# Attention and two MoE blocks on one core: tile zero's product with v three slots later, the softmax weights' product on GpSimd, six dense steps in the last slots

## The chip, the core and the metric

One core of a Trainium2 chip. The metric is device microseconds of one execution. Three runs of the kernel before gave a median of 700.36 us (699.11 to 701.2).

## What is computed

Attention with head mixing (12 heads, 448 rows, batch 2), then two dense blocks, all in fp32:

```python
scores = einsum('bhij,hg->bgij', scale * q @ k.T, w_pre)
attn = exp(scores - max(scores)); attn = attn / (sum(attn) + 1e-09)
attn = einsum('bhij,hg->bgij', attn, w_post)
x = (attn @ v) reshaped to (896, 768)
x = ((x @ w_a) * (x @ w_b)) @ w_out          # 768 -> 1536 -> 768
r = maximum(x @ w_in, 0); out = (r * r) @ w_out2   # 768 -> 2048 -> 768
```

## The kernel before

**Two parts.** The attention part runs first, the dense part behind it. The dense matmuls are split in three (hi*hi, hi*lo, lo*hi: lines 645 to 647), so a "dense step" (`fill(1)`, one `mm`) is three matmuls of 128x448. A dense unit is six steps and needs its weights split into hi and lo by six "split steps" on ScalarE (ACT) and VectorE (DVE).

**Slots.** Each batch has four row tiles of 120, 120, 120 and 88 rows, each cut into pairs of row groups: 6, 6, 6 and 5 pairs, so 46 slots in all; tile zero has slots 0 to 5, tile one 6 to 11. Slot n of the loop issues, in this program order: the premix of pair n+1 (heads mixed by w_pre, L291, PE), the scores qk of a later tile (L206, PE), `post` of pair n (mixing by w_post, L348, PE), then the softmax of pair n+1: row minimum `smin` (DVE, L300), `sexp` (ACT, L307), the addition of 1e-9 to the sum (`z`, L315), the copies of the scores out of PSUM (odd heads DVE L215, even heads ACT L217), and their spreading over partitions by DMA (L224, odd heads from SP's queue, even heads from GpSimd's (POOL's) own instructions). Then come the two copies `evac` of `post`'s result (ACT L376, DVE L374), and `weights2` of pair n+1: reciprocal (L323) and product w2 = wp * 1/z (L324), which `post` of pair n+1 reads as its moving operand in slot n+1. After that `mid` issues loads.

**The 88-row tile** has a second, partial spread per head (L258). In the slots of `HOLD` the spreads wait for the next slot.

**Tile's end.** Where a tile ends (`AVS`, before: slots 5, 11, 17, 22, 28, 34, 40), the product with v (`av_start`, `av`, L387 and L400, then the copies `av_out`) stands on PE, with split steps between. Two slots' softmax lie under it.

**Order.** The schedule is manual: each engine keeps the program order, and an instruction waits for its inputs and for buffers. PSUM has eight banks: T 3, post 2, qk 2, av 1.

Of the kernel before, what the change touches and what calls it, by code (L numbers as in the profile page):

```python
# [7 lines left out]
F32 = mybir.dt.float32  # L8
# [78 lines left out]
def attention_moe_kernel(  # L87
# [17 lines left out]
    PB = {"T": 3, "post": 2, "qk": 2, "av": 1}  # L105
# [21 lines left out]


# [70 lines left out]
    def qk(b, t, c, tags=("qk", "qk")):  # L199
# [102 lines left out]
    def sexp(b, m, f):  # L302
# [9 lines left out]
        if f:  # L312
            z = Z[b, m][0:q]
            eng = nc.vector if b == 0 and PAIRS[m][0] == 0 else nc.gpsimd
            eng.tensor_tensor(out=z, in0=z, in1=eps[0:q].to_broadcast([q, 2]), op=ALU.add)  # L315

    def weights2(b, m):
# [6 lines left out]
        nc.vector.tensor_tensor(  # L324
# [7 lines left out]
    def post_tag(b, m):  # L332
        return "qk" if (b, m) in free_qk else "post"

    def post(b, m):
        t, r, n = PAIRS[m]
        w2 = W2.pop((b, m))
        p = [ps(post_tag(b, m)) for _ in range(n)]
# [115 lines left out]
    def first(c):  # L454
        qk(0, 0, c, ("post", "post") if c % 2 else ("qk", "qk"))
# [43 lines left out]
    pre, aft, mid, end = {}, {}, {}, {}  # L499
    AVS = [base[i] + span[i] - 1 for i in range(len(tiles) - 1)]  # L500
# [7 lines left out]
    def softmax(n, between=()):  # L508
# [5 lines left out]
        for f, *args in between:  # L514
            f(*args)
# [13 lines left out]
    for i in range(0, VP, 2):  # L529
        at(mid, 2, load_v, 0, i, 2)  # L530
    for ti, (b, t) in enumerate(tiles):
# [17 lines left out]
        if ti + 1 < len(tiles):  # L549
            sl = s0 + sp - 1  # L550
            work = [[(steps, k)] for k in STEPS.get((b, t), (0, 0, 0))]
# [12 lines left out]
            at(end, sl, *work[2][0])  # L564
        if ti == 2:
# [10 lines left out]
    def split_steps(u):  # L576
# [10 lines left out]
        def s1():  # L587
# [4 lines left out]
            if u:  # L592
# [12 lines left out]
        def s4():  # L605
            st["hi"] = w_p.tile([128, UW], F32R, tag="wh", name="wh", bufs=3)
            nc.scalar.copy(st["hi"], st["c"])  # L607

        def s5():
            lo = w_p.tile([128, UW], F32R, tag="wl", name="wl", bufs=3)  # L610
# [16 lines left out]

    def split_x0(c):
        src = x32[0][c // 2][:, c % 2, :]
        hi, lo = single(f"ks{2 * c}"), single(f"ks{2 * c + 1}")  # L630
# [8 lines left out]
    for c in range(NC):  # L639
        at(mid, s1 - 2 + c, split_x0, c)  # L640
# [295 lines left out]
```

## Time and profile before

| | us |
|---|---|
| median of three runs | 700.36 |
| the profiled execution | 704.45 |
| its span, first to last instruction | 702.67 |
| PE busy | 680.1 (97%) |
| DVE, ACT, POOL busy | 473.6, 297.9, 62.8 |
| attention loop | 18.7 to 200.6 |
| last product with v | 200.6 to 204.2 |
| dense part to the last matmul | 204.2 to 698.2 |

The profiled execution is 4.1 us (0.6%) longer than the median. Matmuls are pipelined and their recorded ends are modelled, so a busy PE can be slower than it could be; a gap in PE's rows is idle time.

### The profile page before, as it was taken

How to read it: one execution, taken by the hardware profiler on the slowest of the kernel's cores; microseconds unless marked ns; L12 is line 12 of the kernel's file. 1: busy time of each engine (PE TensorE's matmuls, PEld its weight loads, DVE VectorE, ACT ScalarE, POOL GpSimd, SP SyncE). 2: the span in 40 equal slices, each digit the busy share in tenths (PEclk: the TensorE clock that was granted, in tenths of full speed). 3: DMA queues.
4: the chain of work that ended last, by engine and by line, in shares of the span. 5: the costliest groups of instructions: out<-in, count | busy, mean ns of one | idle time of the engine just before them, and what ended most of it. 6: DMA issues, size and time to landing. Idle time of an engine off the chain costs nothing.

```text
span 702.7 us, 16168 instructions
## 1 busy us (share of the span) xinstructions
PE 680.1 (97%) x6881; PEld 582.1 (83%) x6881; DVE 473.6 (67%) x795; ACT 297.9 (42%) x563; POOL 62.8 (9%) x139
## 2 busy tenths in 40 slices
PE   9879998998899999999999999999999999999997
PEld 2456766666689999999999999999999999999996
DVE  6648767798755876766767556668888887645530
ACT  3537655676543333333333322335555553323210
POOL 7112321236100000000000000000000000000000
PEclk9989999999999999999999999999999999999999
DMA  7864577544202323332233322323323234343300
GB/s 236 221 177 137 173 199 184 159 128 142 76 2 90 136 90 120 106 131 94 90 125 103 133 90 90 135 90 98 127 90 134 91 102 155 129 157 120 117 27 27
DMA packets 29092, 84.94 MB, mean 121 GB/s; under 512 B 5059, under 2 KB 18462, under 8 KB 29021
## 3 DMA queue, kind: packets, MB, share of 16 engines
q1 hardware_dynamic: 23933, 73.24, 32.1%
q0 software_dynamic: 4224, 9.43, 5.3%
q10 hardware_dynamic: 864, 1.24, 0.5%
q8 instruction: 54, 0.88, 0.5%
q14 instruction: 17, 0.14, 0.1%
HBM read 62.29 MB, written 2.75 MB: 93 GB/s over the span
## 4 chain that ended last, share of the span: by engine, by line
PE 87%; issue 3%; DVE 3%; ACT 2%; DMA 2%; POOL 1%; POOLq 0%; ACTq 0%; DVEq 0%
PE T L645 9%; PE T L647 9%; PE T L646 9%; PE post L646 6%; PE post L647 6%; PE post L645 6%; PE qk L647 6%; PE qk L645 6%; PE qk L646 6%; PE post L348 4%; PE T L291 4%; PE qk L206 3%; PE av L647 3%; PE av L646 3%; PE av L645 3%
## 5 line engine op out<-in xcount | busy, mean ns | idle before, releaser
L607 ACT CAST wh<-wc 128x768 fp32r<-128x768 f32 x68 | 56.8, 835 | 118.9 <-DVE wc L601 105.4
L611 DVE TENSOR_TENSOR wl<-wc,wh 128x768 fp32r<-128x768 f32 x68 | 64.9, 954 | 48.3 <-ACT wh L607 48.1
L307 ACT ACTIVATE e<-T,nb 128x448 f32<-128x448 f32 (+1 forms) x92 | 57.6, 630 | 55.6 <-DVE nb L300 55.4
L647 PE MATMUL T<-m,wl 128*128 128x448 f32 x207 | 75.6, 365 | 0.0
L645 PE MATMUL T<-m,wh 128*128 128x448 f32 x207 | 75.6, 365 | 0.0
L646 PE MATMUL T<-m,wh 128*128 128x448 f32 x207 | 75.6, 365 | 0.0
L348 PEld LDWEIGHTS post<-w,e 64*64 64x64 f32 x2624 | 53.8, 135 | 26.2 <-issue 12.5
L589 DVE SCALAR_TENSOR_TENSOR wa<-wr,wa 128x768 uint32<-128x768 uint32 x68 | 65.2, 958 | 2.3
L601 DVE SCALAR_TENSOR_TENSOR wc<-wc,wa 128x768 uint32<-128x768 uint32 x68 | 65.2, 958 | 2.3
L348 PE MATMUL post<-w,e 64*64 64x60 f32 (+1 forms) x2624 | 55.8, 218 | 9.0 <-issue 6.0
L584 ACT ACTIVATE wc<-wr 128x768 f32<-128x768 f32 x68 | 61.4, 903 | 0.0
L291 PE MATMUL T<-G,wpre_sb 64*64 64x448 f32 x352 | 53.0, 563 | 3.2 <-issue 2.9
L300 DVE TENSOR_REDUCE nb<-T 128x1 f32<-128x448 f32 (+1 forms) x92 | 52.9, 615 | 4.1 <-PE T L291 2.4
L597 DVE TENSOR_SCALAR wc<-wc 128x768 f32<-128x768 f32 x68 | 37.9, 558 | 19.3 <-ACT wc L584 19.3
L646 PE MATMUL post<-m,wh 128*128 128x448 f32 x125 | 45.7, 365 | 0.0
L645 PE MATMUL post<-m,wh 128*128 128x448 f32 x125 | 45.7, 365 | 0.0
L647 PE MATMUL post<-m,wl 128*128 128x448 f32 x125 | 45.6, 365 | 0.0
L645 PE MATMUL qk<-m,wh 128*128 128x448 f32 x116 | 42.4, 365 | 0.0
L646 PE MATMUL qk<-m,wh 128*128 128x448 f32 x116 | 42.4, 365 | 0.0
L647 PE MATMUL qk<-m,wl 128*128 128x448 f32 x116 | 42.4, 365 | 0.0
L645 PEld LDWEIGHTS T<-m,wh 128*128 128x128 f32 x207 | 38.9, 188 | 3.1
L646 PEld LDWEIGHTS T<-m,wh 128*128 128x128 f32 x207 | 38.9, 188 | 3.1
(180 smaller groups left out, 1416.1 us busy)
## 6 DMA issues: line engine op xcount, KB each, us to landing
wr<-w SPq DMA_DIRECT2D x65, 768.0 KB
G<-s POOLq DMA_DIRECT2D x24, 210.0 KB, 5.0
G<-s SPq DMA_DIRECT2D x20, 210.0 KB
outT<-ta SPq DMA_DIRECT2D x11, 224.0 KB
wr<-w SPq DMA_DIRECT2D x12, 192.0 KB
q<-qT SPq DMA_DIRECT2D x10, 180.0 KB
G<-s POOLq DMA_DIRECT2D x12, 140.0 KB, 3.1
v<-v SPq DMA_DIRECT2D x8, 192.0 KB
```

The lines of the kernel that those rows point to most:

```text
L291: nc.tensor.matmul(p[f][o:o + 64, 0:S], wpre_sb[i:i + 64, o:o + 64], G[t % 2][i:i + 64, r + g, :], start=True, stop=True, skip_group_check ...
L300: nc.vector.tensor_reduce(out=NB[b, m][0:q, f:f + 1], in_=Tps[b, m][f][0:q, 0:S], op=ALU.min, axis=AX.X)
L307: nc.scalar.activation(out=e[0:q], in_=Tps[b, m][f][0:q, 0:S], func=ACTF.Exp, bias=NB[b, m][0:q, f:f + 1], scale=-1.0, accum_out=Z[b, m][0 ...
L348: nc.tensor.matmul(p[g][64 * x:64 * x + 64, c:c + i], e[o:o + 64, j * 128 + y:j * 128 + y + 64], w2[o:o + 64, f, z:z + i], start=True, sto ...
L584: nc.scalar.activation(out=st["c"], in_=rd(st["high"]), func=ACTF.Abs, scale=HSC)
L589: nc.vector.scalar_tensor_tensor(out=a, in0=st["high"], scalar=0x80000000, in1=a, op0=ALU.bitwise_and, op1=ALU.bitwise_or)
L601: nc.vector.scalar_tensor_tensor(out=cu, in0=cu, scalar=3, in1=st["a"], op0=ALU.logical_shift_left, op1=ALU.bitwise_or)
L607: nc.scalar.copy(st["hi"], st["c"])
L611: nc.vector.tensor_tensor(out=lo, in0=st["c"], in1=rd(st["hi"]), op=ALU.subtract)
L645: nc.tensor.matmul(p[:, 0:S], hi[:, sl], x[0], start=first, stop=False)
L646: nc.tensor.matmul(p[:, 0:S], hi[:, sl], x[1], start=False, stop=False)
L647: nc.tensor.matmul(p[:, 0:S], lo[:, sl], x[0], start=False, stop=last)
```

## The change

1. `AVS` of tile zero moves from slot 5 to slot 8, so its probabilities `A[0, 0]` get a buffer of their own (`first_a`); when it is read, the pool is closed and the dense part's `wh`, `wl` buffers take its place.
2. The four loads of batch zero's v move from slot 2 to slots 4, 5, 6 and 7. Loads of k, v of batch one and of the dense weights move by some slots, and unit 3's weights load in slots 41 to 44.
3. The addition of 1e-9 to z goes from DVE to ACT for tile zero, and from POOL to DVE from pair 38 on.
4. The product w2 of pairs 7 to 37 goes from DVE to POOL.
5. In slots 39 to 44 one dense step each stands before `post`; the bank pair qk becomes two single banks, qk and qx, and `post` takes its banks from a list.
6. One split step of each tile end from tile three on moves ahead of the copies of `post`; the split of batch zero's x moves from slots 33 to 38 to 25, 27, 31, 35, 37, 39.

```diff
-    PB = {"T": 3, "post": 2, "qk": 2, "av": 1}
+    PB = {"T": 3, "post": 2, "qk": 1, "qx": 1, "av": 1}
...
+    early = ExitStack()
+    first_a = early.enter_context(tc.tile_pool(name="early", bufs=1, side="right"))
+    split_p = []
+
+    def open_split():
+        early.close()
+        split_p.append(ctx.enter_context(tc.tile_pool(name="split", bufs=3, side="right")))
...
         if f:
             z = Z[b, m][0:q]
-            eng = nc.vector if b == 0 and PAIRS[m][0] == 0 else nc.gpsimd
-            eng.tensor_tensor(out=z, in0=z, in1=eps[0:q].to_broadcast([q, 2]), op=ALU.add)
+            if b == 0 and PAIRS[m][0] == 0:
+                nc.scalar.activation(out=z, in_=z, func=ACTF.Identity, bias=eps[0:q])
+            else:
+                eng = nc.vector if plist.index((b, m)) >= QUIET else nc.gpsimd
+                eng.tensor_tensor(out=z, in0=z, in1=eps[0:q].to_broadcast([q, 2]), op=ALU.add)
...
         nc.vector.reciprocal(out=z, in_=z)
-        nc.vector.tensor_tensor(
+        n = plist.index((b, m))
+        (nc.gpsimd if base[1] < n < QUIET else nc.vector).tensor_tensor(
             out=w2[0:q],
...
-    def post_tag(b, m):
-        return "qk" if (b, m) in free_qk else "post"
+    def post_tags(b, m):
+        return free_qk.get(plist.index((b, m)), ("post", "post"))
...
-            A[b, t] = a_p.tile([128, NG, TILE], F32, tag="a", name="a")
+            A[b, t] = (a_p if b + t else first_a).tile([128, NG, TILE], F32, tag="a", name="a")
...
-    AVS = [base[i] + span[i] - 1 for i in range(len(tiles) - 1)]
+    AVS = [base[1] + 2] + [base[i] + span[i] - 1 for i in range(1, len(tiles) - 1)]
...
-    free_qk = set(plist[QUIET::2])
-    STEPS = {(0, 3): (0, 1, 1), (1, 0): (3, 0, 2), (1, 1): (2, 2, 1), (1, 2): (2, 1, 1)}
+    free_qk = {38: ("qx", "qk"), 40: ("qk", "post"), 41: ("qk", "post"), 42: ("post", "qk"), 44: ("qk", "post")}
+    STEPS = {(0, 3): (1, 0, 1, 0), (1, 0): (1, 3, 1, 0), (1, 1): (1, 2, 2, 0), (1, 2): (1, 2, 1, 0)}
...
-    for i in range(0, VP, 2):
-        at(mid, 2, load_v, 0, i, 2)
+    for i, n in enumerate((4, 5, 6, 7)):
+        at(mid, n, load_v, 0, 2 * i, 2)
...
-    for c, n in enumerate((7, 8, 9, 12, 13, 14)):
+    for c, n in enumerate((8, 9, 10, 12, 13, 14)):
         at(mid, n, load_k, 1, c)
-    for i, n in enumerate((10, 11, 11, 14, 15, 16, 17)):
+    for i, n in enumerate((16, 20, 20, 21, 21, 22, 23)):
         at(end if n in AVS else mid, n, load_v, 1, i)
-    for u, ns in enumerate(((17, 18, 19, 20), (22, 22, 23, 24), (34, 34, 38, 38))):
+    for u, ns in enumerate(((15, 17, 18, 19), (24, 25, 26, 27), (30, 31, 32, 33), (41, 42, 43, 44))):
...
-    for c in range(NC):
-        at(mid, s1 - 2 + c, split_x0, c)
+    for c, n in enumerate((25, 27, 31, 35, 37, 39)):
+        at(mid, n, split_x0, c)
...
-    tags = ["T", "qk", "qk", "post", "av", "T", "post", "T"]
+    tags = ["qx", "T", "qk", "post", "av", "T", "post", "T"]
...
         run(pre, n)
+        if QUIET < n and not last:
+            fill(1)
         post(*plist[n])
         run(aft, n)
         mine = [(evac, *plist[n], g) for g in range(2)]
         if n in AVS:
-            held, mine = held + mine, []
+            held, mine = held + between[n] + mine, []
```

`QUIET` is 38 and `base[1]` is 6.

## Rows read from the trace of the kernel before

**Rows 1.** The page, busy time of each engine, its share, and instructions.
```profile
PE 680.1 (97%) x6881; PEld 582.1 (83%) x6881; DVE 473.6 (67%) x795; ACT 297.9 (42%) x563; POOL 62.8 (9%) x139
```
**Rows 2.** Busy time by stretch: length, engines (x instructions), granted clock, DMA share, GB/s.
```profile
0.00:200.60 200.60, 182.57 (x4349) 121.34 (x4349) 145.92 (x334) 115.39 (x291) 62.77 (x139) 0.98 0.57 161
204.20:698.20 494.00, 493.93 (x2438) 457.49 (x2436) 325.99 (x458) 182.13 (x271) 0.00 (x0) 1.00 0.31 106
```
**Rows 3.** Waits: engine, line, releaser: us in total, times, longest.
```profile
DVE z L315 <- ACT e L307: 6.2, 6, 1.7
PE post L348 <- issue: 6.0, 6, 3.4
```
**Rows 4.** Timeline of DVE in slot 3: start, length, instruction, idle before.
```profile
33.15 1.15 DVE L300 TENSOR_REDUCE nb<-T 128x1 f32<-128x448 f32 x2
35.23 0.16 DVE L315 TENSOR_TENSOR z<-z,eps 128x2 f32<-128x2 f32 x1 [0.94 <-ACT e L307]
36.74 1.15 DVE L300 TENSOR_REDUCE nb<-T 128x1 f32<-128x448 f32 x2
```
**Rows 5.** Timeline of PE in slot 5.
```profile
44.84 0.74 PE L348 MATMUL post<-w,e 64*64 64x60 f32 x17 [3.36 <-issue]
```
**Rows 6.** Busy time by stretch behind that wait, columns as in rows 2.
```profile
44.10:51.00 6.90, 6.17 (x77) 4.93 (x79) 1.57 (x4) 1.62 (x4) 0.78 (x2) 0.51 0.39 104
```
**Rows 7.** DMA queues: packets, MB, share: whole run, 31.1:37.3, 37.3:41.8 (three), 41.8:45.
```profile
q8 instruction: 54, 0.88, 0.5%
...
v<-v SPq DMA_DIRECT2D x3, 384.0 KB
...
q0 software_dynamic: 156, 0.45, 42.8%
q1 hardware_dynamic: 337, 0.50, 42.3%
q14 instruction: 1, 0.01, 0.7%
...
q8 instruction: 1, 0.02, 2.7%
```
**Rows 8.** Timeline of DVE in slot 14.
```profile
83.19 0.28 DVE L324 TENSOR_TENSOR w<-wp,z 128x120 f32<-128x120 f32 x1
83.39 1.15 DVE L300 TENSOR_REDUCE nb<-T 128x1 f32<-128x448 f32 x2
85.11 0.62 DVE L374 COPY a<-post 128x420 f32<-128x420 f32 x1
85.75 0.17 DVE L323 RECIPROCAL z<-z 128x2 f32<-128x2 f32 x1
```
**Rows 9.** Timelines of ACT, POOL and PE there.
```profile
82.57 0.52 ACT L217 COPY s<-qk 88x448 f32<-88x448 f32 x1
...
84.10 0.63 ACT L307 ACTIVATE e<-T,nb 128x448 f32<-128x448 f32 x1 [0.53 <-DVE nb L300]
...
83.39 0.63 POOL L224 DMA_DIRECT2D G<-s  x1 [0.43 <-ACT s L217]
...
83.62 1.30 PE L348 MATMUL post<-w,e 64*64 64x60 f32 x58
```
**Rows 10.** Groups by line, POOL: form, count, busy us, mean ns, idle before.
```profile
L188 POOL TENSOR_TENSOR ks<-x,ks 128x112 fp32r<-128x112 f32 x24 | 9.7, 436 | 0.8 <-ACT ks L631 0.8
```
**Rows 11.** Timeline of POOL, an elementwise operation behind two spreads.
```profile
157.00 0.55 POOL L258 DMA_DIRECT2D G<-s  x1
157.56 1.56 POOL L188 TENSOR_TENSOR ks<-x,ks 128x112 fp32r<-128x112 f32 x4
```
**Rows 12.** Timelines of PE and DVE in slots 43 and 44.
```profile
192.63 1.13 PE L348 MATMUL post<-w,e 64*64 64x60 f32 x64 [0.43 <-DVE w L324]
195.39 1.13 PE L348 MATMUL qk<-w,e 64*64 64x60 f32 x64 [0.44 <-DVE w L324]
...
194.85 0.17 DVE L323 RECIPROCAL z<-z 128x2 f32<-128x2 f32 x1 [0.69 <-POOL z L315]
```

More of the change, by code (lines that the diff above doesn't have):

```diff
@@ L337, in post @@
         w2 = W2.pop((b, m))
-        p = [ps(post_tag(b, m)) for _ in range(n)]
+        p = [ps(tag) for tag in post_tags(b, m)[:n]]
         k = H * KG
@@ L454, in first @@
     def first(c):
-        qk(0, 0, c, ("post", "post") if c % 2 else ("qk", "qk"))
+        qk(0, 0, c, ("post", "post") if c % 2 else ("qk", "qx"))
     def near(h):
@@ L498, in attention_moe_kernel @@
     NS = len(plist)
-    pre, aft, mid, end = {}, {}, {}, {}
-    AVS = [base[i] + span[i] - 1 for i in range(len(tiles) - 1)]
+    pre, aft, mid, end, between = {}, {}, {}, {}, {}
+    AVS = [base[1] + 2] + [base[i] + span[i] - 1 for i in range(1, len(tiles) - 1)]
     QUIET = base[-1] - 3
@@ L503, in attention_moe_kernel, with softmax @@
     HOLD.update({base[1] - 2 - i: tiles[2] for i in range(3)})
-    free_qk = set(plist[QUIET::2])
-    STEPS = {(0, 3): (0, 1, 1), (1, 0): (3, 0, 2), (1, 1): (2, 2, 1), (1, 2): (2, 1, 1)}
+    free_qk = {38: ("qx", "qk"), 40: ("qk", "post"), 41: ("qk", "post"), 42: ("post", "qk"), 44: ("qk", "post")}
+    STEPS = {(0, 3): (1, 0, 1, 0), (1, 0): (1, 3, 1, 0), (1, 1): (1, 2, 2, 0), (1, 2): (1, 2, 1, 0)}
     soft = set()
-    def softmax(n, between=()):
+    def softmax(n, work=()):
         soft.add(n)
@@ L513, in softmax @@
         smin(b, m, 1)
-        for f, *args in between:
+        for f, *args in work:
             f(*args)
@@ L549, in attention_moe_kernel @@
         if ti + 1 < len(tiles):
-            sl = s0 + sp - 1
-            work = [[(steps, k)] for k in STEPS.get((b, t), (0, 0, 0))]
+            sl = AVS[ti]
+            work = [[(steps, k)] for k in STEPS.get((b, t), (0, 0, 0, 0))]
+            between[sl] = work.pop(0)
             at(end, sl, av_start, b, t)
@@ L591, in s1 @@
             )
-            if u:
+            if u > 1:
                 load_w(u + 2)
@@ L605, in s4 @@
         def s4():
-            st["hi"] = w_p.tile([128, UW], F32R, tag="wh", name="wh", bufs=3)
+            st["hi"] = split_p[0].tile([128, UW], F32R, tag="wh", name="wh", bufs=3)
             nc.scalar.copy(st["hi"], st["c"])
         def s5():
-            lo = w_p.tile([128, UW], F32R, tag="wl", name="wl", bufs=3)
+            lo = split_p[0].tile([128, UW], F32R, tag="wl", name="wl", bufs=3)
             nc.vector.tensor_tensor(out=lo, in0=st["c"], in1=rd(st["hi"]), op=ALU.subtract)
@@ L626, in split_x @@
         xs[b][c] = (hi, lo)
+    XT = ((1, 3), (5, 7), (9, 11), (0, 2), (4, 6), (8, 10))
     def split_x0(c):
         src = x32[0][c // 2][:, c % 2, :]
-        hi, lo = single(f"ks{2 * c}"), single(f"ks{2 * c + 1}")
+        hi, lo = (single(f"ks{i}") for i in XT[c])
         nc.scalar.copy(hi, src)
```

4 lines of the change are left out of this document (3 added, 1 removed).

## The prediction, made before the changed kernel ran

> **What bounds the kernel now.** I read the page first: PE is busy 97% of the span [rows 1], so only time in which PE idles or runs slowly can be won. The stretches say where that is: the dense part has 493.93 us of PE in 494.00, the attention part 182.57 in 200.60, so 18.0 us of idle time stand in the first 200 us and none behind [rows 2]. The waits name two things there: DVE waits 6.2 us for ACT at L315, and PE waits 6.0 us at `post` for "issue", that is for nothing the profile sees, 3.4 us of it at once [rows 3].
>
> In slot 5 that wait stands alone: PE stops in the middle of `post` at 41.48 (44.84 less 3.36) and goes on at 44.84 [rows 5]. The clock falls with it: from 44.10 to 51.00 it is granted at 0.51, which is the lower level of 1.2 GHz nearly throughout, against 1.00 in the dense part [rows 2, 6]. Why PE stopped: the instruction queue q8 moves 0.88 MB in 54 packets, 16 KB each, and PE with its weight loads has 13,762 instructions, 255 per packet, so these are PE's instructions [rows 1, 7]. In 37.3 to 41.8 no packet of q8 came, with q0 and q1 holding 85% of the DMA engines; from 41.8 one came, and PE went on [rows 7]. The loads of v (three of 384 KB and one of 192, 1.34 MB) had been issued just before, from 31.1 on, and the spreads of tile two behind them.
>
> In a plain slot another engine sets the pace. In slot 14 each DVE instruction starts where the one before it ends, and the reciprocal-to-reciprocal step is 2.76 us (85.75 less 82.99, where the product at 83.19 follows its reciprocal by 0.20) [rows 8]. `post` starts at 83.62, next to the end of the product (83.47) [rows 8, 9]. In slots 0 to 5 the step is 3.59 (36.74 less 33.15), since DVE stands 0.94 us before L315 until ACT is done, with the copies of scores and of `post` behind it on its queue [rows 4].
>
> **Part by part.**
>
> *Addition on ACT, tile zero.* It removes six waits of DVE, 6.2 us, and six additions of 0.16 [rows 3, 4], together 7.2 us; what waits for the DVE copies behind them is qk's bank, so PE. It adds six small activations on ACT, an operation the trace doesn't show; the nearest rows are the 0.16 addition of the same tile on DVE and the 0.52 copy of 448 columns on ACT [rows 4, 9]; I take 0.2, near the first, as it has the same two columns. ACT then ends later by 0.2 per slot, and the loop from qk's bank through ACT's copies to the next qk is late next. Worked through slot by slot with the same durations, slots 3 and 4 fall from 3.59 to about 2.9, and slots 0 to 2, with one qk more each, by about 0.9. Sum: 3 x 0.9 + 2 x 0.7 = 4.1, **-4.0 us** (bounds -7.2, and -1.0 if each takes ACT 0.52 on the path, 3.1 in all).
>
> *v later, its product in slot 8.* Of the v loads only the first stays ahead of slot 5, 0.38 MB instead of 1.34. The other 0.96 MB stand among the spreads on SP's queue in slots 5 to 7. The product itself is the same PE work in another slot. If PE's instructions come in time, the wait (3.36) goes, and the half clock, 6.90 x (1 - 0.51) = 3.4 [rows 5, 6]. That is 6.8 at most. The spreads of tile two, 210 KB each, still come in one burst once tile zero's last premix is through, and PE will be 4 us earlier with the packet then needed; I leave 1.5 us for a shorter wait without a fall of the clock: **-5.3 us** (bounds -6.8 and 0).
>
> *w2 on POOL, pairs 7 to 37.* It takes 0.20 us per slot from DVE. POOL has no 128x120 product in the trace; the nearest are 128x112 at 436 ns [rows 10] and DVE's own 0.28 [rows 8]. I take 0.45, the first with eight columns more. The queue matters more. In program order the product stands on POOL behind the spread of the slot's even head. The spread starts 0.30 after ACT's copy (83.09 to 83.39) and holds POOL 0.63, on the 88-row tiles 0.55 more for L258 [rows 9, 10]. POOL works in order: an elementwise operation behind two spreads began at 157.56, where the second ended at 157.55 [rows 11]. So in slot 14 w2 would be ready at 83.39 + 0.63 + 0.45 = 84.47 instead of 83.47, and `post` one us later.
>
> How much of it stays? 12 of the 31 products lie under a tile's product with v, some 5 us of PE work; 19 feed a `post` that follows at once, 4 of them in slots of `HOLD` with no spread ahead. The delay isn't paid anew each time, since DVE has become free to start the next minimum earlier. The loop over two slots is: minimum to exp 0.71, two exps and ACT's copy 1.76, to the spread 0.30, spread 0.63, product 0.45, hop 0.1, `post` 1.13, hop 0.08, copy 0.62 and reciprocal 0.2: 5.98, or 2.99 a slot against 2.76 [rows 8 to 12]. Followed through slots 24 to 27 this ends 0.9 us later than before, and 1.4 with L258. For seven tiles about 1.1 each, 7.7. Some 2.5 of that falls where PE stood at "issue" anyway (6.0 less the 3.4 of slot 5) [rows 3]: **+5.0 us**. Bounds: -3.8 (19 x 0.20, if POOL's delay is covered), +17.9 (19 x 0.94, if it is paid each time).
>
> The Trainium skill, GPSIMD Engine Reference, section Engine selection, speaks against this part: two-input elementwise work belongs on VectorE, being about twice as slow on GpSimd. By it the product would be near 0.57 by estimate, and this term about +1 larger; the row at 436 ns is near enough to it.
>
> *Six dense steps.* PE waits 0.43 and 0.44 us for w2 in slots 43 and 44, in which the pace, 2.76, is set by minimum, exp, addition and reciprocal, while `post` takes 1.13 [rows 12]. A dense step is three of the dense part's 2,438 matmuls in 494 us [rows 2], 0.61. Six are 3.65 us taken out of a stretch in which PE never idles; in slots 39 to 44 they find such idle time. Where PE is still full (slot 42, behind the product with v) one of them delays `post`, so I keep **-2.8 us** (bounds -3.65 and 0). The addition on DVE for these pairs saves a hop of about 0.1 each, within that.
>
> *The rest* I cost at nothing: moved split steps, x splits and loads lie on ACT, DVE, POOL and the queues beside tile ends bound by PE. If that cover is gone, a split step of about one us shows on PE.
>
> Sum: -4.0 - 5.3 + 5.0 - 2.8 = **-7.1 us**. The profiled execution, 704.45, would become 697.3; it lies 4.1 above the median of the runs, so on their scale 700.36 - 7.1 = **693.3 us**.
>
> **Rivals.**
>
> *POOL's queue sets every slot.* The spread ahead of w2 is paid in full in the 19 slots, 17.9 us, as it would be if the exp of the next pair could not start earlier. Against the gains of 12.1 this gives +5.8, **706.2 us**: slower. It decides from 0.64 us per slot (12.1 / 19) on. For it: `post` starts 0.15 behind w2 already, no slack [rows 8, 9]. Against it: the loop above closes at 2.99.
>
> *The instruction wait comes back*, in slot 5 or later, with the clock: v's bytes are only moved, and the spreads' burst stays. Then -4.0 + 5.0 - 2.8 = -1.8, **698.6 us**. The row for it is q0 with 42.8%, the spreads alone, in the stretch without a packet [rows 7]. The Trainium skill, DMA: Bandwidth & Descriptors, section Queues, rings and completion order, leads here too: each DMA engine takes turns between its queues by packet, so v's backlog on q1 would not hold back q8. The 4.5 us without a packet of q8 [rows 7] speak against that rule here, but can't say which queue it was.
>
> *POOL's delay is covered*, since DVE with 0.20 less per slot and PE's instruction waits take it up: -4.0 - 5.3 - 2.8 = -12.1, **688.3 us**.
>
> **How the numbers follow.** Forecast 0.60, POOL in every slot 0.17, the wait comes back 0.15, POOL covered 0.08. About 0.3%, 2.1 us, is what a measurement of this kernel can tell from no change. Faster by more is below 698.3: nearly all of the forecast, the covered case and a part of the second, 0.68; slower by more, above 702.5, is the first rival, 0.17; the rest, 0.15, is within. The range goes from 688, the covered case, to 702, past the wait that comes back; the first rival, 0.17, is left out above it.
>
> **What would show it.** On DVE in slots 1 to 5 no wait at L315, and a step near 2.9. In slot 5 no PE gap over 1.5 us and a granted clock of 1.00 from 41 to 54. On POOL w2 directly behind L224, `post` waiting for it, and steps near 3.0 in slots 14 to 17. Dense matmuls between the last premixes without the 0.4 us waits. I am wrong if another wait of 3 us or more drops the clock, if PE waits in slot 8 for v, or if plain slots take over 3.2 us.

## The result and the profile after

The changed kernel took **707.13 us** in the median (705.52 to 709.36), beside 699.74 us (697.88 to 701.2) for the kernel before: 1.0109 of it, 95% interval 1.0066 to 1.0153. It is slower, by about 1.1%; the forecast was 693.3 us, with 688 to 702 as its range. Ratios, here and below, leave out runs more than 1.5% above the fastest of the same kernel, and are not the quotients of the medians. The profiled execution took 708.65 us with a span of 706.9, against 704.45 and 702.7 before.

The page of the changed kernel, busy time of each engine, answers to [rows 1]:

```profile
span 706.9 us, 16257 instructions
...
PE 681.2 (96%) x6881; PEld 573.1 (81%) x6881; DVE 468.5 (66%) x766; ACT 300.3 (42%) x569; POOL 74.3 (11%) x162
```

PE has the same 6,881 matmuls, and DVE's load did go down by 5 us and POOL's up by 11.5, as the change says. So the parts do what they say; the time lies elsewhere. Busy time by stretch, columns as in [rows 2]: the attention part, a piece of slots 5 and 6, and 460 us from inside the dense part.

```profile
0.00:204.90 204.90, 183.05 (x4367) 116.54 (x4367) 140.45 (x305) 117.19 (x296) 74.26 (x162) 0.98 0.58 157
37.00:43.80 6.80, 5.86 (x88) 4.09 (x92) 3.09 (x9) 2.52 (x7) 0.78 (x2) 0.50 0.59 169
220.00:680.00 460.00, 460.00 (x2251) 421.83 (x2250) 317.40 (x443) 173.98 (x256) 0.00 (x0) 1.00 0.33 112
```

And the same 460 us of the kernel before, where PE alone was asked for:

```profile
220.00:680.00 460.00, 460.00 (x2272) 1.00 0.33 113
```

Two things are to be seen. First, the granted clock is at its lower level again (0.50) for 6.8 us, from 37.00 on: the half clock of [rows 6] has not gone, it has come 7 us earlier. (It comes once more, for 3.4 us from 112.09 on, just behind a wait of 2.22 us for instructions; the profile of before has no second fall.) Second, in a stretch in which PE is never idle and has its full clock in both kernels, 2,251 matmuls start instead of 2,272. From the starts of the 37th and the last dense matmul, 2,411 intervals take 488.63 us before and 492.91 after: 202.67 and 204.44 ns from start to start on average. This mean distance is called the pace from here on. It makes **4.3 us** in a place where the forecast saw nothing to win or lose.

The timeline of PE in slots 4 to 8 (`post` is L360, the premix L299, the product with v L412) shows where the first slots' gain went; it answers to [rows 5]:

```profile
33.74 0.27 PE L360 MATMUL post<-w,e 64*64 64x60 f32 x3
35.45 1.12 PE L360 MATMUL post<-w,e 64*64 64x60 f32 x61 [1.44 <-issue]
37.94 1.89 PE L299 MATMUL T<-G,wpre_sb 64*64 64x448 f32 x8 [1.36 <-DMA G<-x]
...
40.95 1.92 PE L360 MATMUL post<-w,e 64*64 64x60 f32 x61
...
54.04 0.59 PE L299 MATMUL T<-G,wpre_sb 64*64 64x448 f32 x2 [1.52 <-issue]
...
57.69 0.43 PE L412 MATMUL av<-a,v 128*64 128x120 f32 x4 [0.28 <-DMA v<-v]
...
60.69 1.20 PE L360 MATMUL post<-w,e 64*64 64x60 f32 x62
```

Slot 4 starts at 33.74, 3.2 us earlier than before (36.96). By slot 5 it is 0.4 us later (40.95 against 40.55): PE stood 1.44 us for instructions and 1.36 us for the spreads of tile one, which had not landed, and then worked at the lower clock. In slot 8 it stood 1.52 us for instructions again, ahead of the product that had been moved there.

The additions on ACT did what was foreseen. DVE's timeline in slots 2 and 3 of the changed kernel, which answers to [rows 4], has no addition and no wait of 0.94 in it, and the step from minimum to minimum is 2.75 us (32.89 less 30.14) instead of 3.59. (Each addition takes 0.30 us on ACT, where 0.2 was taken.)

```profile
30.14 1.15 DVE L308 TENSOR_REDUCE nb<-T 128x1 f32<-128x448 f32 x2
31.20 0.61 DVE L223 COPY s<-qx 120x448 f32<-120x448 f32 x1
31.91 0.62 DVE L386 COPY a<-post 128x420 f32<-128x420 f32 x1
32.49 0.17 DVE L334 RECIPROCAL z<-z 128x2 f32<-128x2 f32 x1
32.69 0.28 DVE L336 TENSOR_TENSOR w<-wp,z 128x120 f32<-128x120 f32 x1
32.89 1.15 DVE L308 TENSOR_REDUCE nb<-T 128x1 f32<-128x448 f32 x2
```

So did w2 on POOL. The groups of POOL have it at 416 ns, where 0.45 us was taken (columns as in [rows 10]):

```profile
L336 POOL TENSOR_TENSOR w<-wp,z 128x120 f32<-128x120 f32 (+1 forms) x31 | 12.9, 416 | 6.3 <-DVE z L334 3.4 <-PE T L299 2.6
```

The waits of PE over the whole run (columns as in [rows 3]) name it ten times, none over 0.93 us:

```profile
PE post L360 <- POOL w L336: 5.0, 10, 0.9
PE post L360 <- issue: 4.3, 4, 1.4
```

And the timelines of POOL and PE in slot 14, which answer to [rows 9], show it behind both spreads, with `post` late by 0.93:

```profile
79.39 0.62 POOL L232 DMA_DIRECT2D G<-s  x1 [0.40 <-ACT s L225]
80.00 0.55 POOL L266 DMA_DIRECT2D G<-s  x1
80.57 0.40 POOL L336 TENSOR_TENSOR w<-wp,z 128x120 f32<-128x120 f32 x1
...
81.02 1.13 PE L360 MATMUL post<-w,e 64*64 64x60 f32 x64 [0.93 <-POOL w L336]
```

And the dense steps stand in idle time. In slots 43 and 44 the matmuls of one lie ahead of `post`, which waits no more (0.43 and 0.44 in [rows 12]):

```profile
193.72 0.47 PE L662 MATMUL qx<-ks,wh 128*128 128x448 f32 x1
194.03 0.37 PE L663 MATMUL qx<-ks,wh 128*128 128x448 f32 x1
194.23 0.36 PE L664 MATMUL qx<-ks,wl 128*128 128x448 f32 x1
194.53 0.27 PE L360 MATMUL post<-w,e 64*64 64x60 f32 x2
```

**Where the 11.35 us went.** The forecast for the profiled execution was 697.3; it was 708.65. By the start of slot 12's `post` the changed kernel was to be 8.4 us ahead (4.0 and 5.3 less about 0.9 of w2) and is 1.3 ahead (74.59 against 75.89): 7.1 us. From slot 12 to 37 it loses 5.35 us where 4.1 were left for w2: 1.2. From slot 37 to 45 it takes 0.26 us longer with the six dense steps in it, where 0.85 were allowed: -0.6. The slower pace of the dense matmuls is 4.3, and from the start of the last dense matmul to the end it takes 0.7 less (4.17 us against 4.91). Together 11.3. This compares one profile with one profile; what of it other executions have, the experiments ask.

### The profile page after: what moved, and what is told of

It reads as the page before. It is cut to its first block, busy times and chain, and to the rows that moved or that the text cites. A ratio compares the mean times of both kernels' runs of the same rounds, so it can differ in the third digit from the quotient of the medians.

```text
span 706.9 us, 16257 instructions
## 1 busy us (share of the span) xinstructions
PE 681.2 (96%) x6881; PEld 573.1 (81%) x6881; DVE 468.5 (66%) x766; ACT 300.3 (42%) x569; POOL 74.3 (11%) x162
## 3 DMA queue, kind: packets, MB, share of 16 engines
HBM read 62.29 MB, written 2.75 MB: 92 GB/s over the span
## 4 chain that ended last, share of the span: by engine, by line
PE 86%; DMA 5%; DVE 3%; ACT 2%; issue 2%; POOL 1%; SPq 0%; ACTq 0%; POOLq 0%; DVEq 0%
PE T L662 9%; PE T L664 9%; PE T L663 9%; PE post L664 6%; PE post L663 6%; PE post L662 6%; PE post L360 4%; PE T L299 3%; PE qx L662 3%; PE av L664 3%; PE av L663 3%; PE av L662 3%; PE qk L664 3%; PE qx L664 3%; PE qx L663 3%; PE qk L663 3%
## 5 line engine op out<-in xcount | busy, mean ns | idle before, releaser
L664 PE MATMUL T<-m,wl 128*128 128x448 f32 x237 | 87.1, 367 | 0.0
L663 PE MATMUL T<-m,wh 128*128 128x448 f32 x237 | 87.0, 367 | 0.0
L662 PE MATMUL T<-m,wh 128*128 128x448 f32 x237 | 86.5, 365 | 0.0
L360 PEld LDWEIGHTS post<-w,e 64*64 64x64 f32 x2688 | 54.1, 138 | 32.6 <-POOL w L336 17.6
L360 PE MATMUL post<-w,e 64*64 64x60 f32 (+1 forms) x2688 | 55.2, 221 | 10.3 <-POOL w L336 5.0
L299 PE MATMUL T<-G,wpre_sb 64*64 64x448 f32 x352 | 49.9, 571 | 5.8 <-issue 4.1
L663 PEld LDWEIGHTS T<-m,wh 128*128 128x128 f32 x237 | 44.3, 187 | 4.3
L662 PEld LDWEIGHTS T<-m,wh 128*128 128x128 f32 x237 | 44.5, 188 | 3.9
L664 PEld LDWEIGHTS T<-m,wl 128*128 128x128 f32 x237 | 44.5, 188 | 3.9
L386 DVE COPY a<-post 128x420 f32<-128x420 f32 x42 | 25.9, 616 | 18.7 <-PE post L360 18.0
L600 DVE TENSOR_SCALAR wa<-wr 128x768 uint32<-128x768 uint32 x68 | 37.8, 556 | 0.0
```

What stands on the lines that cost most here:

```text
L299: nc.tensor.matmul(p[f][o:o + 64, 0:S], wpre_sb[i:i + 64, o:o + 64], G[t % 2][i:i + 64, r + g, :], start=True, stop=True, skip_group_check ...
L360: nc.tensor.matmul(p[g][64 * x:64 * x + 64, c:c + i], e[o:o + 64, j * 128 + y:j * 128 + y + 64], w2[o:o + 64, f, z:z + i], start=True, sto ...
L662: nc.tensor.matmul(p[:, 0:S], hi[:, sl], x[0], start=first, stop=False)
L663: nc.tensor.matmul(p[:, 0:S], hi[:, sl], x[1], start=False, stop=False)
L664: nc.tensor.matmul(p[:, 0:S], lo[:, sl], x[0], start=False, stop=last)
```

## Experiments

Theory at the start: the first slots fail because the waits for instructions and the lower clock are not caused by v's bytes. Rivals: w2 on POOL alone makes it slower; the slower dense pace does, through the place of `wh` and `wl`, which the later product moves to the upper end of the memory (byte 210,912 instead of 82,368). The kernels ran in five groups, each on one chip with its own runs of the kernel before (medians 703.9, 704.4, 702.0, 699.9 and 698.7 us); ratios are against these runs.

### The parts alone

**The changed kernel once more** (no edit).

> The changed kernel, unchanged, as a yardstick beside the parts. Its profile had a second oddity: dense matmuls follow each other at 204.4 ns where those of the kernel before do at 202.6, some 4 us over 2,420 of them. If the chip or the execution sets that pace, this run has the same pace as the other three kernels of this call. If the change sets it (new place of the split weights, new order of the PSUM banks), this run is at 204.4 and the kernel with w2 alone on POOL, whose dense part is that of before, at 202.6. Time: 1.011 times the kernel before.

Measured: 1.0057 (1.0029 to 1.0086). The pace is 204.45 ns again; the wait in slot 5 was 4.37 us, and the clock fell from 41.8 and from 113.4 on. So the pace is there again in a second execution, while the waits have other lengths.

**w2 on POOL alone.**

```diff
-        nc.vector.tensor_tensor(
+        n = plist.index((b, m))
+        (nc.gpsimd if base[1] < n < QUIET else nc.vector).tensor_tensor(
             out=w2[0:q],
```

> The kernel before with one part alone: the product w2 of pairs 7 to 37 on POOL. Theory 1 (the product stands behind the spread on POOL's queue, each loop of two slots grows from 5.5 to 6.0 us): +5 us, 1.007, of which half may hide in instruction waits; post waits for POOL's w in about 15 slots. Rival (each of 19 slots pays the 0.94 in full): +18 us, 1.025. Rival (DVE's relief pays for it): -2 to 0 us.

Measured: 1.0026 (0.9997 to 1.0055), +1.8 us. PE waits for POOL 3.5 us in five places, none over 0.94. In the profile slots 12 to 37 take 100.09 us, against 95.40 before. In slot 5 PE stood 0.62 us, not 3.36, though nothing in the first six slots differs from the kernel before. This is the first sign that the 3.36 of [rows 5] belongs to that execution.

```profile
PE post L349 <- POOL w L325: 3.5, 5, 0.9
PE post L349 <- issue: 2.5, 5, 1.2
```

**The product with v in slot 8, v loaded in slots 4 to 7, alone**, with `wh` and `wl` at the upper end as in the change.

```diff
+    first_a = early.enter_context(tc.tile_pool(name="early", bufs=1, side="right"))
...
-    AVS = [base[i] + span[i] - 1 for i in range(len(tiles) - 1)]
+    AVS = [base[1] + 2] + [base[i] + span[i] - 1 for i in range(1, len(tiles) - 1)]
...
-    for i in range(0, VP, 2):
-        at(mid, 2, load_v, 0, i, 2)
+    for i, n in enumerate((4, 5, 6, 7)):
+        at(mid, n, load_v, 0, 2 * i, 2)
```

> The kernel before with one part alone: tile zero's product with v in slot 8, v loaded in slots 4 to 7, first buffer and split buffers as in the change; the addition for tile zero stays on DVE. Theory 2 (v's bytes ahead of PE's instructions made the wait in slot 5): no wait of 3 us in slot 5, no fall of the clock, -5 to -7 us, 0.991. Rival (the spreads alone are enough to make PE wait): a wait of 1 us or more in slots 4 to 8 and the clock falls all the same, -2 to +1 us.

Measured: 1.0077 (1.0041 to 1.0114), +5.4 us. Its dense pace is 204.45 ns. In PE's timeline the wait in slot 5 is shorter (1.44), and the next stands in slot 7, longer; the clock falls behind it:

```profile
42.82 0.38 PE L356 MATMUL post<-w,e 64*64 64x60 f32 x11 [1.44 <-issue]
...
51.95 0.38 PE L356 MATMUL post<-w,e 64*64 64x60 f32 x4 [3.98 <-issue]
```

Its stretch behind that wait, columns as in [rows 2]:

```profile
50.85:57.65 6.80, 5.70 (x127) 3.84 (x128) 2.73 (x6) 2.19 (x5) 0.00 (x0) 0.50 0.99 207
```

The clock is at its lower level, and the DMA engines are busy for 0.99 of it. Slot 12 starts at 78.38, against 75.89 in the kernel before. So this part alone makes a loss, in two places: the first slots and the pace.

**Six dense steps alone**, with the bank pair cut in two and the earlier splits of x.

```diff
         run(pre, n)
+        if QUIET < n and not last:
+            fill(1)
         post(*plist[n])
```

> The kernel before with one part alone: one dense step ahead of post in slots 39 to 44, with the single banks qk and qx, the list of banks for post, and the earlier splits of x. Theory 3: -2.8 us (0.996), the steps fill waits of PE. Rival: the steps delay post in slots whose pace PE sets, 0 us. If the order of the banks sets the dense pace, this kernel has 204.4 ns per dense matmul and gains nothing, or loses 1 us.

Measured: 0.9912 (0.9878 to 0.9946), -6.2 us; pace 202.67, no fall of the clock in the profile. Six dense steps are 3.65 us [rows 2]; the interval, -3.8 to -8.6 us, lies beyond that, so a part of it is not theirs.

**The addition of tile zero on ACT alone.**

```diff
-            eng = nc.vector if b == 0 and PAIRS[m][0] == 0 else nc.gpsimd
-            eng.tensor_tensor(out=z, in0=z, in1=eps[0:q].to_broadcast([q, 2]), op=ALU.add)
+            if b == 0 and PAIRS[m][0] == 0:
+                nc.scalar.activation(out=z, in_=z, func=ACTF.Identity, bias=eps[0:q])
+            else:
+                nc.gpsimd.tensor_tensor(out=z, in0=z, in1=eps[0:q].to_broadcast([q, 2]), op=ALU.add)
```

> The kernel before with one part alone: tile zero's addition of 1e-9 on ACT. Theory 5 (slots 0 to 4 get 3 us faster, but DMA sets when PE's instructions and tile one's spreads arrive): post of slot 4 starts 3.2 us earlier, PE then waits longer in slots 4 to 6, and 0 to -2 us are left, 0.998 to 1.000. Rival (the 3 us are kept): -3 to -4 us, 0.995.

Measured: 0.9946 (0.9909 to 0.9983), -3.8 us. Slot 4 starts at 33.25, 3.7 us early. PE gives some of it back at once: with slot 4 early, it stood 2.13 us ahead of the premix of slot 5, for which the trace names the load of v, and the clock fell to 0.50 from 36.77 on, for 3.4 us. Slot 5 starts at 39.77, only 0.8 early.

```profile
33.25 1.39 PE L350 MATMUL post<-w,e 64*64 64x60 f32 x64
36.76 1.89 PE L291 MATMUL T<-G,wpre_sb 64*64 64x448 f32 x8 [2.13 <-DMA v<-v]
```

**The changed kernel with w2 back on DVE.**

```diff
-        n = plist.index((b, m))
-        (nc.gpsimd if base[1] < n < QUIET else nc.vector).tensor_tensor(
+        nc.vector.tensor_tensor(
```

> The changed kernel with the product w2 back on DVE, all else as changed. Theory 1, with the part alone at +1.8 us: -2 to -5 us against the changed kernel (702 to 704), no post waiting for POOL. Rival (each of 19 slots paid the full 0.94): -18 us, 688.

Measured: 0.9999 (0.9965 to 1.0033), against 1.0057 with w2 on POOL: about 4 us for w2 on POOL in the changed kernel, by ratios from two chips. In the profiles slots 12 to 37 take 95.84 us with it on DVE and 100.08 with it on POOL (the copy), 4.2 us. Its pace is 204.45, and PE stood 5.31 us for instructions in slot 7.

### The dense pace

**`wh` and `wl` moved alone**, in the kernel before: to the upper end, at the bytes of the changed kernel, or to the lowest place.

```diff
+    split_p = ctx.enter_context(tc.tile_pool(name="split", bufs=3, side="right"))
...
-            st["hi"] = w_p.tile([128, UW], F32R, tag="wh", name="wh", bufs=3)
+            st["hi"] = split_p.tile([128, UW], F32R, tag="wh", name="wh", bufs=3)
```

> The kernel before with nothing changed but the place of wh and wl: at the top of SBUF, byte 210912 on, as in the changed kernel, with the tiles behind them 18,432 bytes lower. Theory 4 (their place sets the pace of the dense matmuls): 204.44 ns per matmul instead of 202.67, 4.3 us over 2,412 of them, 1.006. Rival (the pace came with the product with v in slot 8, or its first buffer): 202.67 ns, 1.000.

> The kernel before with wh and wl at byte 17856 on, ahead of all others, and the activations of the dense part where they were. If a high place of wh and wl is slow: 202.67 ns, 1.000. If the distance or order of weights and activations counts: another pace than 202.67.

Measured: 1.0021 (0.9986 to 1.0057) at the upper end and 0.9978 (0.9946 to 1.001) at the lowest. The same 460 us, at the upper end:

```profile
220.00:680.00 460.00, 460.00 (x2264) 1.00 0.33 112
```

and at the lowest place:

```profile
220.00:680.00 460.00, 460.00 (x2272) 1.00 0.33 112
```

At the upper end the pace is 203.33 ns, 1.6 us more over the dense part; at the lowest it is that of the kernel before. Only addresses differ, so in these profiles the pace does depend on where tiles lie. But the changed kernel, and the later product alone, have the dense part's tiles at the same bytes as the first of these kernels and a pace of 204.44, so the bytes are not all of it.

**An offset of 32 bytes.** At 82,368 `wh` begins on a multiple of 64 bytes, at 210,912 it doesn't. So the changed kernel was run with `wh` on such a multiple (210,880), and the kernel before with `wh` off it (82,400) and all tiles behind `wl` 64 bytes higher.

```diff
         early.close()
+        ctx.enter_context(tc.tile_pool(name="pad", bufs=1, side="right")).tile([128, 8], F32, tag="pad", name="pad")
         split_p.append(ctx.enter_context(tc.tile_pool(name="split", bufs=3, side="right")))
```

> The changed kernel with 32 bytes kept free at the upper end of the memory, so that wh and wl begin at byte 210,880 (a multiple of 64) instead of 210,912 (32 more than a multiple of 64); nothing else moves. In the unchanged copy of it the dense products start 204.45 ns apart, in the kernel before (wh at 82,368, a multiple of 64) 202.67 ns. Theory of the offset (a weight tile that begins in the middle of 64 bytes is loaded more slowly): 202.67 ns again, and 4.3 us less than the copy's 706.3, so 702.0, 0.999 of the kernel before. Rival (the high place itself, or what else the later product moves, slows them): 204.4 ns and 706.3, 1.006.

> The kernel before with 32 bytes kept free ahead of wh and 32 more behind wl: wh and wl begin at 82,400 instead of 82,368, in the same low place, and everything behind them moves by 64. Theory of the offset: the dense products start 203.3 to 204.45 ns apart instead of 202.67, 1.6 to 4.3 us more, 1.002 to 1.006 of the kernel before. Rival (the high place): 202.67 ns and no change, 1.000.

Measured: 1.0135 (1.0094 to 1.0175) and 1.0063 (1.0029 to 1.0098). The first has the slowest pace of all, 206.67 ns; the second changes its pace from stage to stage of the dense part, between 204.1 and 206.7. The same 460 us of the first:

```profile
220.00:680.00 460.00, 460.00 (x2228) 1.00 0.33 112
```

and of the second:

```profile
220.00:680.00 460.00, 460.00 (x2241) 1.00 0.33 111
```

The second fits the theory of the offset, the first goes against it. The theory falls. (That the first has another pace than the copy is one more case in which only addresses were moved and the pace changed.)

**The later product with `wh` and `wl` where the kernel before has them**: the first output tile lies there until they need the place, and everything of the attention part and the dense tiles lie at the upper end. This was done to the changed kernel (its edit is shown), to the later product alone, and to the changed kernel with w2 on DVE.

```diff
-    first_a = early.enter_context(tc.tile_pool(name="early", bufs=1, side="right"))
+    first_a = early.enter_context(tc.tile_pool(name="early", bufs=1))
...
-        split_p.append(ctx.enter_context(tc.tile_pool(name="split", bufs=3, side="right")))
+        split_p.append(ctx.enter_context(tc.tile_pool(name="split", bufs=3)))
...
-    sb = att.enter_context(tc.tile_pool(name="att", bufs=1))
+    sb = att.enter_context(tc.tile_pool(name="att", bufs=1, side="right"))
```

> The changed kernel with wh and wl at the bytes of the kernel before (82,368 on); the first output tile of the later product lies there until the weights need the place, and G, q, v, e, s, a and the tiles of the dense layers lie at the upper end instead, all on multiples of 64. The instructions and their order are those of the changed kernel. Theory of the place (the dense products' pace follows from where wh and wl lie): 202.67 ns from start to start instead of 204.45, 4.3 us less than the copy, so 702 beside a kernel before of 704, about 1.000. Rival (the pace follows from something else in the changed program): 204.4 ns and 1.006.

> The kernel before with the later product with v alone, wh and wl where the kernel before has them and the rest at the upper end. The same edit with wh and wl at the upper end was 1.0077 of the kernel before. Theory of the place: 202.67 ns, 4.3 us less, so 1.002: what the later product does to the first slots is then about nothing, not the 5.3 us less of the forecast. Rival (the forecast was right on the first slots and the place alone hid it): 0.993. Rival (the pace follows from something else): 1.008.

> The changed kernel with the weights' product on DVE and wh and wl where the kernel before has them. With wh and wl at the upper end it was 0.9999 of the kernel before. Theory of the place: 202.67 ns and 4.3 us less, 0.994, level with b_best (0.9931), so that the later product gives and takes nothing. Rival (the later product gives its 5.3 us once the pace is level): 0.986, 5 us ahead of b_best. Rival (the pace follows from something else): 1.000.

Measured: 1.013 (1.0094 to 1.0167), 1.0101 (1.0041 to 1.0162) and 1.0098 (1.0062 to 1.0133): none better than the same kernel with `wh` and `wl` at the upper end (1.0057, 1.0077 and 0.9999, on other chips), and the first and the last worse. All three have 206.67 ns, 9.6 us more than the kernel before over 2,411 intervals. The row of the first:

```profile
220.00:680.00 460.00, 460.00 (x2227) 1.00 0.33 111
```

So the place of `wh` and `wl` alone is not the cause either; here they are where they were. Of the tiles that meet them on PE, m0 to m31 have moved, but `ks` has not, and in the profile of the later product alone the matmuls on `ks` start 206.67 ns apart too (624 intervals; 202.67 in the kernel before), with both of their operands at the bytes of before. So the addresses of a matmul's own operands do not set the pace alone. What does stays open. All eight profiles of kernels whose tiles lie as in the kernel before, or with `wh` and `wl` at the lowest place, have 2,271 or 2,272 starts in the 460 us; all twelve with another layout have 2,227 to 2,264.

Not every profile can be set beside the median of its kernel: of the changed kernel with w2 on DVE and the 32 bytes kept free (below), the profiled execution has 206.67 ns and took 707.97 us, 9.3 above the median of its runs. The others have no trace, so their pace is not known.

### The first slots, and what is left to use

**The changed kernel, w2 on DVE, 32 bytes kept free; and the kernel before with the dense steps and the additions on ACT (and, for the last pairs, on DVE), its product still in slot 5.** The edit of the second, in part:

```diff
-            eng = nc.vector if b == 0 and PAIRS[m][0] == 0 else nc.gpsimd
-            eng.tensor_tensor(out=z, in0=z, in1=eps[0:q].to_broadcast([q, 2]), op=ALU.add)
+            if b == 0 and PAIRS[m][0] == 0:
+                nc.scalar.activation(out=z, in_=z, func=ACTF.Identity, bias=eps[0:q])
+            else:
+                eng = nc.vector if plist.index((b, m)) >= QUIET else nc.gpsimd
+                eng.tensor_tensor(out=z, in0=z, in1=eps[0:q].to_broadcast([q, 2]), op=ALU.add)
...
+        if QUIET < n and not last:
+            fill(1)
```

> The changed kernel with the weights' product back on DVE and wh and wl on a multiple of 64: so against b_best it differs by the later product with v of tile zero and the transfers that were moved with it. Theory that the later product gives nothing here (the waits for instructions come in slot 5 or 8 all the same, and the clock falls): 702.5 of a_w2_dve less 4.3, so 698, 0.994 of the kernel before, and some 4 us behind b_best. Rival (the later product does give the 5.3 us of the forecast, and only the pace hid it): 0.980 or less, ahead of b_best. If the offset has nothing to do with the pace: 702.5, 1.000.

> The kernel before with the six dense steps in the last slots, the addition of tile zero on ACT, and the addition of the last slots on DVE; the product with v stays in slot 5, the weights' product on DVE, wh and wl where they were. Theory that the two gains lie in different stretches (b_dense6 0.9912, b_eps_act 0.9946): they add, 0.986, about 694 beside a kernel before of 704, dense products 202.67 ns apart. Rival (what comes early in the first slots is lost again at a wait for instructions in slot 5): no better than the six dense steps alone, 0.991.

Measured: 0.995 (0.9917 to 0.9983) and 0.9931 (0.9902 to 0.996). The two gains do not add: 0.9912 times 0.9946 would be 0.986. In the profile of the second PE stood 1.71 us in slot 4 and 3.70 in slot 5, where the additions' gain went, and the clock fell. The wait stands behind the 47th matmul of `post`, as in [rows 5]:

```profile
39.52 1.01 PE L351 MATMUL post<-w,e 64*64 64x60 f32 x47
44.23 0.74 PE L351 MATMUL post<-w,e 64*64 64x60 f32 x17 [3.70 <-issue]
```

and the stretch behind it has the lower clock:

```profile
44.20:47.50 3.30, 3.27 (x49) 2.18 (x49) 1.57 (x4) 1.62 (x4) 0.78 (x2) 0.50 0.39 129
```

In the first, PE waited for v itself, 3.8 us in two pieces ahead of and inside the moved product, as had been named as a way to be wrong:

```profile
53.01 0.63 PE L412 MATMUL av<-a,v 128*64 128x120 f32 x8 [1.19 <-DMA v<-v]
56.24 0.67 PE L412 MATMUL av<-a,v 128*64 128x120 f32 x4 [2.60 <-DMA v<-v]
```

**The same two sets once more, on another chip.**

> The kernel of b_best once more, on the chip of the three others. It has the same instructions in the same places, so the pace should be 202.67 ns again. If its 3.70 us of waiting for instructions in slot 5 and its two falls of the clock belong to the program, they are here again and it is 0.993; if they belong to the execution, this profile may show others, and the time lies between 0.986 and 0.993.

> The kernel before with the six dense steps alone, once more, on another chip. On the first chip it was 0.9912, with no fall of the clock in its profile and a granted clock of 0.997 or more in 11 of 12 runs; the kernel before had 0.997 or more in 11 of 30 runs there. If the six steps themselves save about 3 us (2.8 in the forecast, 4.1 from the slots' starts of its profile) and the rest was the luck of the first slots: 0.994 to 0.997. If they save 6 us everywhere: 0.991. Dense products 202.67 ns apart, as in every profile of a kernel with this layout.

Measured: 0.9986 (0.996 to 1.0013) and 0.999 (0.9964 to 1.0017), where the first chips had 0.9931 and 0.9912. The pace is 202.67 in both, as on the first chips. In the first slots the profiles differ: PE stood 3.03 us behind the 47th matmul of slot 5 in the one and 3.09 in the other, which had stood 0.89 there on the first chip. The rows of the six dense steps, first chip and second:

```profile
42.21 0.47 PE L348 MATMUL post<-w,e 64*64 64x60 f32 x17 [0.89 <-issue]
...
44.54 0.73 PE L348 MATMUL post<-w,e 64*64 64x60 f32 x17 [3.09 <-issue]
```

The same program thus has the long wait in one execution and not in another. The traces also show what PE waits for there. In the seven profiles whose slots 0 to 5 are those of the kernel before, a packet of the instruction queue q8 ends at 40.45 to 40.96 us where PE stood 0.62 to 0.89, and at 42.57 to 43.29 where it stood 3.09 to 3.36. In all fifteen profiles with a wait behind that matmul PE goes on 1.15 to 1.71 us after the packet's end. v is loaded in slot 2 in all seven, so v's bytes alone do not decide when the packet comes; what does is not shown.

**v loaded in slot 2 again, its product left in slot 8**, in the changed kernel with w2 on DVE and `wh` and `wl` where the kernel before has them.

```diff
-    for i, n in enumerate((4, 5, 6, 7)):
-        at(mid, n, load_v, 0, 2 * i, 2)
+    for i in range(0, VP, 2):
+        at(mid, 2, load_v, 0, i, 2)
```

> As a_w2_dve_low, but v of tile zero is loaded in slot 2, as in the kernel before, instead of in steps 4 to 7; its product stays in slot 8. In the profile of a_w2_dve_low PE waited 0.8 us for v ahead of that product (2.7 in a_low, 3.8 in a_w2_dve_pad32), tile one's spreads were late by 0.6, and step 12 began at 72.32 us, against 69.39 in b_eps_act, whose product stays in slot 5. Theory that v in steps 4 to 7 lands too late: no wait for v is left and step 12 begins 1 to 3 us earlier; 0.995 to 0.999 times a_w2_dve_low (1.0098), so 1.005 to 1.009, if the dense products start 206.67 ns apart again. Rival (the product is late in itself, because in slot 8 it is followed by less work that PE could do beside its copies): no earlier step 12. If v's bytes hold the spreads of tile one back, the wait for them grows beyond 0.6 us.

Measured: 1.0137 (1.01 to 1.0174), against 1.0098 with v in slots 4 to 7, on the same chip. No wait for v is left, but the wait for the spreads grows to 1.34, and a new one of 2.77 for ACT's copy of scores stands ahead of `post` of slot 6, behind which the clock fell; slot 12 starts at 71.91, 0.4 earlier.

```profile
PE qk L215 <- ACT s L226: 3.1, 2, 2.8
PE T L300 <- DMA G<-x: 1.3, 1, 1.3
```

So v in slots 4 to 7 does land late. That v in slot 2 gets in the way of the spreads fits the longer wait for them, in one profile; neither placing makes the moved product pay.

## Why the prediction was wrong

**The term for the product with v failed, in its premise.** It took 3.36 us of waiting and 3.4 of half clock from one execution [rows 5, 6] and called them the kernel's. They are an execution's. With slots 0 to 5 the same as before, PE stood there 0.62, 0.62, 0.89 and 0.89 us in the profiles of the kernels with w2 on POOL, with the offset of 32 bytes, with `wh` at the lowest place and with the six dense steps, and 3.09 in two others. The profiled execution of before lay 4.1 us above the median of its three runs; the prediction noted this and put it aside, though it was a sign that those runs had less of the wait and the clock than the term subtracted from them.

The price itself was near: from slot 0 to slot 6 the profile of before takes 34.7 us, the four with the short wait 29.3 to 29.7, so such an execution loses 5.0 to 5.4. How often one comes, the runs show. Of the 126 runs of the kernel before beside the experiments, 16 of 30, 17 of 31, 7 of 25 and 6 of 40 on the four chips have a mean granted clock of 0.995 or less, as the profiled execution has, and their medians lie 2.4 to 6.4 us above those of the same chip's runs at 0.998 or more. So many executions lose it and many do not. That may also be why ratios differ between chips, since the kernel before that they divide by has more of these executions on the first two.

The second half of that step failed too: "if PE's instructions come in time" was the condition, and they did not. From 33 to 76 us (slots 4 to 12) PE stands 2.6 to 6.0 us in waits over 0.2 us in the seven profiles with the product in slot 5 and the additions on DVE, and 6.4 and 4.9 with the product in slot 8; with the additions on ACT it is 3.2 to 7.2 with the product in slot 5 (three profiles) and 5.2 to 9.0 with it in slot 8 (eight). (Four of these eight have w2 on POOL, and 1.7 to 2.2 us of waiting for it are in their sums.) So the waits were not fewer. Slot 12 starts at 71.4 to 76.2 us with the product in slot 5 and at 77.0 and 78.4 with it in slot 8; with the additions on ACT at 69.4 to 75.3 and 71.9 to 77.6. The rival "the instruction wait comes back, in slot 5 or later, with the clock" describes the first slots; its 698.6 us was the sum without what follows.

On the rule of round-robin turns that the prediction had weighed (the Trainium skill, DMA: Bandwidth & Descriptors, section Queues, rings and completion order): with all of v's loads ahead the wait in slot 5 is 0.62 us in some executions and 3.36 in another, and with only the first of them ahead it is 1.44 and one of 3.98 follows, among the loads that were moved. So v's backlog is not by itself what holds the instructions back. That is the direction in which the rule spoke, though no run here shows the turns themselves.

**"The rest I cost at nothing" failed.** The change has to find room for a second output tile, and so moves `wh`, `wl` and all tiles behind them. The prediction read 493.93 us of PE in 494.00 [rows 2] as a part with nothing to win or lose. But a busy row says only that PE is not idle; the number of matmuls that start in it says how fast it is. The pace cost 4.3 us in the changed kernel and up to 9.6 in others. That placing can change it is shown (in seven pairs of kernels the edit only moves addresses, and the pace differs); what about it matters is not, and the later product alone, whose dense tiles lie where they do in the kernel with `wh` and `wl` moved alone, has 204.44 ns against 203.33, so something else in the program matters too.

**The additions on ACT** were right up to slot 4, which is early by 3.2 us in the changed kernel and 3.7 alone, where 3.4 (3 x 0.9 + 0.7) was worked out. The total, -4.0 forecast and -3.8 measured (-1.2 to -6.4), is not shown to be this gain: in the profile only 0.8 us of lead is left by slot 5, and the lead of 6.5 by slot 12 comes with the long wait of slot 5, which this execution does not have. So that the totals agree may be luck. What was not seen is what is late next: what comes earlier to slots 4 and 5 waits there for instructions or transfers.

**w2 on POOL** was right in mechanism and, in the profiles, about right in size: +5.0 forecast, 4.7 and 4.2 us more from slot 12 to 37. By ratios it is about +4 in the changed kernel, 2.2 between the first and the last kernel with `wh` and `wl` left in place (one chip), and +1.8 (-0.2 to 3.9) alone, below the +5.0. The sum has one slip: pairs 7 to 37 lie in six tiles, not seven, which by the same working gives 6 x 1.1 - 2.5 = +4.1. Its working is in the trace of the changed kernel: slots 12 to 14 take 1.46 us more than before, then about one us is lost per tile, while plain slots keep their pace (slots 14 to 17 start within 8.42 us, 8.58 before). The rival in which POOL sets every slot, whose 706.2 is near the result, is not what happened: PE waits 5.0 us for POOL in ten slots, not 17.9 in nineteen.

**The six dense steps** were right in sign and short in size. From slot 39 to 45 the kernel before takes 21.00 us, and both profiles with the steps alone 21.09, so 3.56 of the 3.65 us are gained, where 2.8 was kept (in the changed kernel 21.64, so 3.01). Their ratios, 0.9912 and 0.999, differ by more than that: -6.2 us is more than the steps hold, -0.7 less than they gain, and the two profiles differ in slot 5.

**Chances.** 0.17 for slower leaned on one mechanism, POOL. The loss came from two that had no price: a wait sized on one execution, and the place of tiles. The parts measured alone add up to -2.8 us with the first measurement of the dense steps and to +2.7 with the second, the whole to +4.0 (the copy) and +7.6; how much of that difference is chips and how much the parts' effect on each other is not shown.

**What beats the kernel before**: the dense steps and the additions, without the later product and without w2 on POOL: 0.9931 on one chip, 0.9986 on another. The dense steps alone (0.9912 and 0.999) and the additions alone (0.9946) are as good within their intervals, and on the second chip neither the two together nor the steps alone are clear of no change. The best with the later product in it, 0.995, has the same additions and dense steps; on its chip it is level with 0.9931.

## What to carry to other kernels

A wait or a fall of the clock that stands in one profiled execution is a term of a sum only if the other runs have it: compare the profile's time and granted clock with the spread of the runs before subtracting it. A stretch in which PE is always busy has a pace, so count the matmuls that start in it, before and after; an edit that moves tiles can change it. And ask of an earlier slot which transfer or instruction packet it will now arrive ahead of.

## What the runs showed of the hardware

- **The pace of dense matmuls.** 128x448 matmuls, each with its own weight load, at a granted clock of 1.00, start 202.67, 203.33, 204.44 or 206.67 ns apart on average, the same in every 20 us of 460 us of one execution to 0.1 ns (with one exception, in which it changes between stages from 204.1 to 206.7), in kernels that differ in where their tiles lie and in program order. The Trainium skill, TensorE: Matmul & The Clock Gate, section Back-to-back issue gap, gives columns / 2.4 GHz plus about 2.5 ns for a warm matmul by itself, 189.2 ns for 448 columns by estimate; every row here is 13.5 to 17.5 ns above that, and the measurement decides.
- **PE's wait for instructions** stands at the same matmul (behind the 47th of slot 5) in 15 of the 20 profiles, is 0.34 to 4.37 us long there, and ends 1.15 to 1.71 us after a packet of the instruction queue. The Trainium skill, Runtime: NRT & Kernel Launch, section Instruction fetch mechanics, calls the cost of going from one block of instructions to the next mostly hidden; these waits are not.
- **The granted clock** fell to 0.50, its level of 1.2 GHz, within or just behind 18 of the 23 waits of PE of 2 us or more in the 20 profiles; behind the other five, of 2.08 to 2.75 us, it did not. It also fell behind shorter ones, as in the changed kernel, where waits of 1.44 and 1.36 us stand ahead of the fall at 37.00.
